# Linear attention with a Fourier mix and an MLP on one core: single PSUM banks, fixed rings, transposes by DMA for two batches, and a new order

## The chip, the core and the metric

The kernel runs on one core of one Trainium2 chip. A core has five engines that run their own instruction streams: TensorE (PE in the profile), VectorE (DVE), ScalarE (ACT), GpSimd (POOL) and SyncE (SP), and 16 DMA engines that they share. The metric is the time of one execution on the device in microseconds; the median of the runs is compared. Lower is better.

## What is computed

The reference is a linear attention with a decaying state, then a Fourier mix over sequence and width, a normalisation and an MLP with residual. Batch B = 4, H = 8 heads, S = 768 tokens, D = 48, so a width of 384; the MLP is 1536 wide.

```python
for t in range(S):                              # per batch and head
    cur = einsum('bhd,bhe->bhde', u[None] * kt, vt)
    y[:, :, t] = einsum('bhd,bhde->bhe', rt, state + cur)
    state = w[None, :, :, None] * state + einsum('bhd,bhe->bhde', kt, vt)
...
X = np.real(fft(fft(x, axis=1), axis=2))        # x: y with the heads side by side
u = x + X
un = (u - mean(u)) / sqrt(var(u) + 1e-06)
out = u + maximum(un @ w_ch1, 0) @ w_ch2
```

Inputs r, k, v, w, u and both weights are f32, and so is the output.

## The kernel before

**Attention.** The tokens are cut into 24 chunks of 128, six to a batch. For chunk i, `load` brings k, r and v from HBM as [128 tokens, 8 heads, 48], so each contiguous run is 192 bytes (lines 270, 274, 276). `attend` multiplies k and r by powers of the decay (KR, line 290), turns k and r from token-major to feature-major with eight PE transposes (line 302) into one PSUM tile and copies this to SBUF (KRT, line 305 on ACT or 306 on DVE), forms products for the bonus term u (PR, line 307), the scores (A_ps, line 317), their causal mask (MA, on POOL after an ACT copy, lines 324 and 326, or on DVE, line 329), the state update (u_ps, line 349; Sst, lines 361 and 363), and in yd_ps the bonus (line 381), the carried state (line 386) and the masked scores by V (line 403). DE (line 392) and TT (POOL, line 394) make the bonus term; it joins either through PE (line 409) and an ACT copy, or in the DVE addition (line 412). The result of a chunk is X. The state carries from chunk to chunk inside a batch.

**Fourier.** For batch 0 the halves of X are folded chunk by chunk (`narrow`, lines 426 and 433), for the other batches once all six chunks are there (`fold`, lines 449, 455, 463: each EO and HH is one DVE instruction over three chunks). `fourier` multiplies by tables of cosines (te, tn; line 495), copies to SBUF (TT2, lines 504 and 507), reverses (TR, line 514), multiplies by the second table (line 533), adds X (UF: by a PE matmul with the identity, line 544, and ACT, line 552, or in one DVE instruction, line 546), rescales (UB, lines 555 and 559) and gathers the statistics (lines 563 and 565). A batch has two halves of three blocks. UB is turned to UNT: for batch 0 by PE (line 574), for the others by a DMA transpose issued from SP (line 601).

**MLP.** There are eight halves `hf`. `mlp1` makes twelve PSUM tiles of three matmuls each (line 618), each passed through the ReLU to HT by ACT (line 623) or DVE (line 626). `mlp2` makes three tiles of twelve matmuls (line 638), added to UF on DVE (osb, line 646) and written out from POOL (line 650). W1 and W2 are read as f32 and cast to bf16 by six DMAs issued from POOL (line 671), W1 after X of chunk 3 and W2 after X of chunk 5.

**Order.** `op` records every step with the engine or engines that can do it. `ORDER`, a string written out in the kernel, lists numbers of these steps, with `.1` where the second engine is taken. `emit` issues them in that sequence, so each engine's own stream, and SP's and POOL's queues of DMAs too, run in the order of the string. SP issues the loads one after the other, and a load waits where its buffer is not yet free. 150 `idle` matmuls are declared and 40 are listed (line 198); they only keep PE busy. PSUM has eight banks, shared out as rings: `mm` 3, `A_ps` 2, `tp`, `u_ps` and `yd_ps` one each (with `tp` of two kilobytes). SBUF tiles come from pools with a number of buffers each.

Of the kernel before, what the change touches and what calls it, by code (L numbers as in the profile page):

```python
# [11 lines left out]
AX = mybir.AxisListType  # L12
# [3 lines left out]
B = 4  # L16
H = 8
S = 768
D = 48
# [4 lines left out]
NP = H // 2  # L24
CH = 98

# [25 lines left out]
class _Tile:  # L52

    def __init__(self, source, ring, bufs):
        self.source, self.ring, self.bufs = source, ring, bufs
        self.value = None
# [5 lines left out]
class _Schedule:  # L62

    def __init__(self):
        self.ops = []

    def tile(self, source, ring, bufs):
        return _Tile(source, ring, bufs)

    def op(self, name, eng, ns, fn, r=(), w=(), new=(), use=(), after=(), dma=0, pri=0, port=False, other=(), fill=False,  # L70
           link=None, uses=None, fixed=False):
        alts = [(eng, ns, port, fn)] + list(other)
        self.ops.append(dict(name=name, alts=alts, deps=list(r), after=list(after), w=list(w), new=list(new),
                             use=list(use), dma=dma, pri=pri, fill=fill, n=len(self.ops), link=link,
                             uses=uses or [[] for _ in alts], fixed=fixed))

    def emit(self, order):
        counts = {}
        for n, a in order:
            o = self.ops[n]  # L80
            for t in o["new"]:
                if isinstance(t.source, list):
                    m = counts.get(t.ring, 0)
                    counts[t.ring] = m + 1
                    t.value = t.source[m % t.bufs]
                else:
                    pool, shape, dtype, name = t.source
                    t.value = pool.tile(shape, dtype, name=name, bufs=t.bufs)
            o["alts"][a][3]()
# [3 lines left out]
154 153 194 150 155 168 157 160 162 195 151 161 159 196 169 177 156 188 199 176 174 197 191 175 163 158 200 178 173 170 171 198 180 172 164 201 179  # L93
165 202 182 166 203 152 181 167 0 205 183 1 271 206 2 184 211 273 190 185 193 186 293 187 204 3 207 4 274.1 5 208 272.1 294 295 275 209 276 296.1 212
283 281 277.1 279 6 297 7 216 8 282.1 278.1 280 9 10 210 284 315 298 268 303 269 11 301.1 299 302.1 285 317 214 304.1 12 318.1 215 300 287 286 13 288
320 337 305 321.1 323 14 15 16 316 192 324 339 217 189 306 325 322.1 338 307 218 17 18 340 19 326 213 309.1 308 319 219 347 310.1 341 342 359 348.1
327 345.1 343.1 20 21 328 346.1 329 361 22 344.1 362 331.1 330 23 381 24 332.1 364 402 349 360.1 220 367.1 383 363 350 365 221 369 368.1 351 25 26 270
231 27 384.1 366 353.1 352 222 386 385 354.1 226 289 28 312 370.1 387.1 389.1 371 1006 334 227 290 29 311 30 372 388.1 31 373 32 33 390.1 34 1007
375.1 374 333 35 291 376.1 36 1005 335 37 292 391 378 377 743 355 757 392 764 356 313 336 382 358 380 225 379 357 420 314 393 765 766 228 767 768 744
401 395 394 745 746 747 758 759 396 223 403 411 397 1009 224 760 404 398 761 400 399 1008 419 748 769 762 749 1010 406 770.1 763 229 750 751 409.1 752  # L100
405 753 412.1 230 754 755 410.1 421 756 429 413 422.1 407 773 774.1 771 779 414 775.1 772 424 780 781 415 785 776 427.1 799 786 787 811 408 782 800
812.1 417.1 801 805 813.1 416 806 807 795 788 793 794 796.1 797 798 425 38 39 802.1 1011 418.1 808.1 428.1 426 819 814 1017 456.1 820.1 423 1012 437
431 1018 823 1033 432 824 438 232 439 433 1034.1 821 474 233 1027 440.1 435 822.1 1015 1028 455 1035 1016 442 1036 441 1039 443.1 444.1 445 1037 492
1019 446 1040.1 1038 434 240 1013 1020.1 430.1 237 1051 436 1014 246 447 1052.1 449 1049 243 450 448 451 1023 1050 783 465 1024 457 473 466.1 1025
453.1 458.1 241 452 1026 1029 235 454.1 459 460 777 1030 236 475 461.1 463.1 778 467 242 784 476 1021 462.1 1061 491 1022 1031 1062 1043 477 247 1032
464.1 248 468 493 515 478 494 1044 552.1 238 481 495 239 1055 789 469 479 234 790 809 496 791 482 471 470 792 480 499.1 1056 1045 497 570 472 498 1053
534 1057 1046 485 1054 252 1041 815 1058 486 483 487 1067 1042.1 484.1 803 489.1 488 804 816 1068 810 490.1 533 817 501 588 1065 818 1069 502 267 503
1063 1066 500.1 255 517 1064 1070 505 1059 518.1 504 1047 1060 506 520 1048 507 535 523.1 521 1091 508 536 509 1092 516 510 258 1079 1093 522 511 1080
1094 512 513 1103 1081 514 1082 1104 551 825 829 1105 826 827 830 831 828.1 1106 837 838 832 839 553 524.1 840 833 834 841 835 554 538 836.1 525 541.1
842 843 526.1 844.1 519 855 537 849 845.1 856 857 850.1 527 543 851.1 864 846.1 876 858 852.1 870 544 871.1 877.1 528 863 865.1 539 605 561 866.1  # L110
542.1 529 607 878.1 556 867.1 531 872.1 879.1 530 559.1 560.1 540 557 1073 532 873 1071 558 1075 884 1072.1 1074 545 1076 562 1099 546 1077 555 1100
569 1087 1078 1083 1088 847 547 579 244 1084 1107 580 245 608 1085 1108.1 250 1095 859 1086 251 571 1096.1 1097 253 549.1 572.1 548 1098 254 1119
550.1 587 262 574 1120 563 263 1101 573 575 256 853 589 564 577 565 1089 257 1102.1 1111 590.1 1090 576 567 566 1115 1112 591 630 568 578 592 264 848
854 581 860 593.1 595 594.1 1116 582 609 861 1127 862 583 1117 874 596 585 584 1128 648 586 1118 720 880 599 249 1135 1129 600 601 261 1133 1136 868
1113 1134 1130 869 603 602 881 1114.1 1137 1109 604 1138 597 875 1125 606 1110.1 610 684 598 1123 882 647 613 615 1139 616 611 883 614 1124.1 1126
1140 617 612 619.1 1121 1141 618 629 1131 1122 1142 620.1 1175 259 1132 621 631 260 622 1176 265 632 623 266 1163 1177 624 1178 634 1164 637.1 638.1
635 625 1151 1165 636 628 1152 1166 626 627 639 649 1153 640.1 885 886 633 1154 887 650 897 898 888.1 899 889 890 900.1 891 657 641 892 893 651 894
895 652 642 901 896 683 655 903 904.1 909 902 905.1 915 643 910 911 916.1 685 917.1 906.1 645 644 924 912.1 653 930 918.1 931.1 666.1 923 936 686 646
654 937.1 925.1 659 665 926.1 688 932.1 687 667 927.1 938.1 668.1 656 1143 939 669 1147 919 1144 1145 1148.1 660 1155 661 1146 658 1159 1156 701 663
675 691 1149 1173 689 1150.1 692 662 1174 670 690 664 1160 703 676 677 673 1161 704.1 678 1169 671 679 1162.1 1157 1170 705 681 706 1158 913 672 1167  # L120
709 907 674 1199 1168 908 710 914 707 920 680 934 1171 921 708 682 1187 933 922 702 1172.1 944 695 719 1200 696 940 697 721 693 722.1 699 698 694.1
1188 1201 711 700 1202 724 712.1 1189 713 727.1 725.1 1179 714 728.1 715 1195 1180 726.1 1181 1196 1190 717 716 723 1197 1182 718 1185 1198 928 729
1191 1186.1 730 731 1211 1192.1 929 733 935 732 941 1212 942 734 735 1183 1205 1213 1184 736 1206 1203 1214 1193 1204 737 1209 1194 738 1207 1210 1247
739 1208 741 1248 742 740 943 945 957 1249 946 947 958 959 1250 948.1 949 950 960 951 953 954 952.1 955 1235 956 961 962 1236 963 1237 964.1 975 965.1
969 1238 976 977 970.1 1223 971.1 966.1 978.1 972.1 984 967 996 983 985 997.1 1224 986 998.1 988 987 1225 999 989 990 1226 979 991.1 1215 968 992.1
1000 1243 1216 993.1 1221 994 1004 1244 1245 995 1222 1217 980 973 1246 1231 974 1218 1233 1001 1232.1 981 1227 1002 1234.1 1219 1228 1003 1251 982
1220 1253 1252 1265 1254 1239 1266 1267 1240 1269 1268 1241 1270 1281 1242 1229 1282 1275 1230 1279 1276 1255 1280 1271 1256.1 1257 1272 1258 1283
1273 1274 1284 1277 1285 1263 1278 1286 1259 1264 1287 1291 1260 1292 1261 1262 1288 1293 1294 1295 1289 1290 1296 1297 1298
"""


def _order(sch):
    return [(int(t.split(".")[0]), int(t.split(".")[1]) if "." in t else 0) for t in ORDER.split()]


@with_exitstack
def kernel(
    ctx: ExitStack,
# [54 lines left out]
    def new(pool, shape, dtype, name, bufs):  # L193
        return sch.tile((pool, shape, dtype, name), name, bufs)
# [524 lines left out]
```

## Time and profile before

| what | value |
|---|---|
| median of 3 runs | 198.49 us (198.18 to 200.11) |
| span of the profiled execution | 196.4 us, first to last instruction |
| median less span | 2.1 us |
| PE busy | 170.4 us, 87% |
| DVE busy | 148.6 us, 76% |
| ACT busy | 112.2 us, 57% |
| POOL busy | 60.5 us, 31% |
| granted PE clock, mean | 0.982 |
| HBM read, written | 20.03 MB, 4.72 MB |

The profile gives its own execution by the span; what lies around it is taken as the 2.1 us between the span and the median. A group of instructions is shown as line, engine, operation, output and inputs, shape and count, then busy us and mean ns of one, then the engine's idle time ahead of it and what ended that. The row of slices gives tenths of busy time in 40 equal pieces of the span. In the table by stretches each engine has its busy us and, in brackets, its instructions. A chain of waits is followed back from the last instruction; each piece is a start, a length and what it was.

### The profile page before, as it was taken

The numbers are of one execution on the slowest core, as the hardware profiler recorded it, in microseconds if no ns is written. First come the engines' busy times: TensorE is split into PE (matmuls) and PEld (weight loads), VectorE is DVE, ScalarE is ACT, GpSimd is POOL, SyncE is SP. The second block draws the span as 40 slices with busy tenths as digits, with TensorE's granted clock in tenths as the row PEclk, the third lists the DMA queues.
The fourth block names the chain that finished last, engine by engine and source line by source line (L and its number), as shares of the span: only waits on it lengthen the run. The fifth ranks groups of instructions, "written<-read, shape, count | busy, mean of one in ns | idle before, by whom it ended". The sixth has DMA issues, their size and how long they took to land.

```text
span 196.4 us, 4461 instructions
## 1 busy us (share of the span) xinstructions
PE 170.4 (87%) x1711; PEld 113.8 (58%) x1711; DVE 148.6 (76%) x334; ACT 112.2 (57%) x263; POOL 60.5 (31%) x90
## 2 busy tenths in 40 slices
PE   0698993399699999997999999979999998899990
PEld 0355651387467666685566665866676576555650
DVE  7789994167889998989898979998888969702140
ACT  3956650259687767168765643786934526693100
POOL 5034260333211453315126253434724111000131
PEclk9999999669999999999999999999999999999999
DMA  5999999899998994323799455230032114400221
GB/s 99 202 213 216 249 178 218 173 186 189 189 220 165 205 216 101 82 83 62 141 194 198 136 122 122 80 60 3 2 63 80 40 43 100 100 0 3 80 105 55
DMA packets 86404, 24.43 MB, mean 124 GB/s; under 512 B 82928, under 2 KB 84592, under 8 KB 86384
## 3 DMA queue, kind: packets, MB, share of 16 engines
q1 hardware_dynamic: 81520, 16.69, 43.8%
q0 software_dynamic: 3680, 7.08, 13.8%
q10 hardware_dynamic: 1184, 0.39, 1.0%
q8 instruction: 13, 0.21, 0.5%
q14 instruction: 7, 0.06, 0.1%
HBM read 20.03 MB, written 4.72 MB: 126 GB/s over the span
## 4 chain that ended last, share of the span: by engine, by line
PE 49%; DMA 20%; issue 19%; POOL 3%; DVE 3%; ACT 2%; SPq 1%; POOLq 0%; DVEq 0%
PE mm L618 15%; PE mm L638 14%; DMA vt<-in_v_dram 11%; PE tp L302 5%; DMA UNT<-UB 3%; DMA kr<-in_r_dram 3%; PE mm L495 3%; PE A_ps L317 3%; DMA te_t<-te_c 3%; POOL out_dram L650 2%; PE yd_ps L403 2%; PE mm L533 2%; PE u_ps L349 1%; PE yd_ps L386 1%; DVE KR L290 1%
## 5 line engine op out<-in xcount | busy, mean ns | idle before, releaser
L618 PE MATMUL mm<-UNT,W 128*128 128x384 bf16 x288 | 53.5, 326 | 2.6 <-DMA UNT<-UB 2.6
L638 PE MATMUL mm<-W,HT 128*128 128x384 bf16 x288 | 51.0, 326 | 0.0
L623 ACT ACTIVATE HT<-mm 128x384 bf16<-128x384 f32 x75 | 36.4, 492 | 18.1 <-PE mm L618 18.0
L394 POOL TENSOR_TENSOR TT<-V,DE 128x384 bf16<-128x384 bf16 x24 | 22.8, 951 | 57.1 <-ACT DE L392 28.6
L638 PEld LDWEIGHTS <-HT 128*128 128x128 bf16 x288 | 27.2, 98 | 16.8
L618 PEld LDWEIGHTS <-W 128*128 128x128 bf16 x288 | 26.0, 97 | 18.3 <-DMA UNT<-UB 3.1
L650 POOL DMA_DIRECT2D out_dram<-osb x24 | 13.4, 557 | 48.6 <-DVE osb L646 45.0
L326 POOL TENSOR_SCALAR_AFFINE_SELECT MA<-AC 128x512 bf16<-128x512 bf16 x27 | 18.3, 684 | 25.2 <-ACT AC L324 13.9
L646 DVE SCALAR_TENSOR_TENSOR osb<-mm,rstd,UF 128x384 f32<-128x384 f32 x24 | 14.8, 615 | 12.8 <-PE mm L638 12.3
L290 DVE TENSOR_TENSOR KR<-kr,wtab 128x768 bf16<-128x768 f32 x24 | 23.4, 975 | 0.5 <-DMA kr<-in_r_dram 0.2
L626 DVE TENSOR_SCALAR HT<-mm 128x384 bf16<-128x384 f32 x21 | 11.6, 554 | 9.8 <-PE mm L618 9.5
L324 ACT CAST AC<-A_ps 128x512 bf16<-128x512 f32 x27 | 15.6, 588 | 5.1 <-PE A_ps L317 5.1
L198 PE MATMUL mm<-zero 128*128 128x512 bf16 x40 | 12.6, 416 | 6.8 <-DVE eps_t L231 6.8
L302 PE MATMUL tp<-ident,KR 128*128 128x128 bf16 x192 | 16.0, 231 | 0.9 <-DVE KR L290 0.5
L302 PEld LDWEIGHTS <-KR 128*128 128x128 bf16 x192 | 13.0, 104 | 5.0 <-DVE KR L290 3.2
L412 DVE TENSOR_TENSOR X<-yd_ps,TT 128x384 bf16<-128x384 f32 x15 | 8.3, 553 | 8.5 <-POOL TT L394 6.8
L329 DVE TENSOR_TENSOR MA<-A_ps,mtri 128x512 bf16<-128x512 f32 x21 | 14.0, 680 | 0.6 <-PE A_ps L317 0.5
L305 ACT COPY KRT<-tp 128x1024 bf16<-128x1024 bf16 x11 | 11.1, 1013 | 5.5 <-PE tp L302 5.3
L403 PE MATMUL yd_ps<-V,MA 128*128 128x48 bf16 x192 | 8.8, 184 | 6.2 <-ACT V L296 6.2
L296 ACT CAST V<-vt 128x384 bf16<-128x384 f32 x19 | 9.3, 513 | 8.4 <-DMA vt<-in_v_dram 8.3
L495 PE MATMUL mm<-te_t,XF 128*128 128x193 bf16 x108 | 13.4, 261 | 0.5 <-DVE XF L433 0.5
L403 PEld LDWEIGHTS <-MA 128*128 128x128 bf16 x192 | 8.2, 97 | 9.7 <-issue 7.3
(81 smaller groups left out, 247.7 us busy)
## 6 DMA issues: line engine op xcount, KB each, us to landing
kr<-in_k_dram SPq DMA_DIRECT2D x24, 192.0 KB, 3.9
vt<-in_v_dram SPq DMA_DIRECT2D x24, 192.0 KB, 3.9
out_dram<-osb POOLq DMA_DIRECT2D x24, 192.0 KB, 2.2
kr<-in_r_dram SPq DMA_DIRECT2D x23, 192.0 KB, 3.8
W<-in_moe_w_ch_dram POOLq DMA_DIRECT2D x6, 384.0 KB, 7.6
te_t<-te_c SPq DMA_DIRECT2D x1, 579.0 KB, 5.1
hid_t<-hid_c SPq DMA_DIRECT2D x1, 288.0 KB, 5.2
wrow<-in_w_dram ACTq DMA_DIRECT2D x1, 192.0 KB, 3.8
```

What stands on the lines that cost most here:

```text
L290: op(("KR", i), "DVE", 960, lambda: nc.vector.tensor_tensor(out=KR().rearrange("t s p (a d) -> t (s p) a d", a=2)[:, :, :, 0:D], in0=kr(). ...
L302: nc.tensor.transpose(tp()[:, s, p, :], KR()[:, s, p, :], ident)
L324: op(("AC", i, a), "ACT", 590, lambda: nc.scalar.copy(AC(), A_ps[a]()), r=[("A", i)], w=[("AC", i, a)], new=[AC], use=[A_ps[a]], pri=pri, ...
L326: op(("MA", i, a), "POOL", 630, lambda: nc.gpsimd.affine_select(out=MA[a](), in_=AC(), pattern=[[0, NP], [1, 128]], base=0, channel_multip ...
L394: op(("TT", i), "POOL", 830, lambda: nc.gpsimd.tensor_tensor(out=TT(), in0=V(), in1=DE().unsqueeze(2).to_broadcast([128, H, D]), op=AluOp. ...
L403: nc.tensor.matmul(y[:, h, :], lhsT=MA[a]()[:, p, :], rhs=V()[:, h, :], start=False, stop=(h == H - 1), skip_group_check=True)
L495: nc.tensor.matmul(fp()[:, par, :], lhsT=lhsT[:, g * CH:g * CH + 128], rhs=rhs, start=(nb == 0 and par == 0), stop=(nb == last and par == ...
L618: nc.tensor.matmul(hp(), lhsT=W1[:, dt, ft * 128:(ft + 1) * 128], rhs=UNT()[:, :, dt, :], start=(dt == 0), stop=(dt == 2))
L623: op(("HT", hf, ft), "ACT", 495, lambda: nc.scalar.activation(out=HT()[:, ft, :], in_=hp(), func=Act.Relu, scale=-1.0), r=[("hp", hf, ft)] ...
L638: nc.tensor.matmul(mo(), lhsT=HT()[:, ft, j * 128:(j + 1) * 128], rhs=W2[:, ft, :], start=(ft == 0), stop=(ft == 11))
L646: op(("osb", hf, j), "DVE", 620, lambda: nc.vector.scalar_tensor_tensor(out=osb(), in0=mo(), scalar=rstd()[:, j:j + 1], in1=UF()[:, j, :], ...
L650: op(("out", hf, j), "POOL", 550, lambda: nc.gpsimd.dma_start(out=out[b, row:row + 128, :], in_=osb()), r=[("osb", hf, j)], w=[("out", hf, ...
```

## The change

It does the following.

- All eight PSUM banks are tiles of their own. The order string names a bank for each step that opens a PSUM tile (`150@4`), so any use can take any bank.
- SBUF tiles are rings of fixed tiles; UF goes from 5 to 4 buffers and UNT from 4 to 3.
- Queries of batch 0 are read by two DMAs, one from ACT and one from SP, six tokens to a row (runs of 1152 bytes), in place of six loads. They are scaled by six tables `wtq` (ACT) in two DVE instructions (QR6), turned by 24 PE transposes (`tq6`) and copied to QT6 by four copies (three on ACT, one on DVE). Chunks 0 to 5 then have k only in KR, four transposes and half a KRT copy. QR6 lies in the bytes of W2, and the queries and `wtq` in two of the HT tiles.
- Chunks 12 to 23 (batches 2 and 3) get KRT by a DMA transpose from SP in place of eight PE transposes and a copy.
- W1 is loaded in two blocks of columns, and `mlp1` waits for the block it needs; its place is set by POOL's order alone. W2 may be loaded after `tq6`.
- EO and HH of `fold` are split by chunk, so each pair of chunks can start when it is there. The parts of yd_ps and of `mlp2` (four parts of three matmuls in place of two of six) are steps of their own.
- Outputs go from POOL or from SP: 11 and 13 in the new order.
- Only the padding of KR is set to zero; some of these go to POOL.
- `ORDER` is another string. Choices in it: KRT copies on DVE 4 (13), masks on DVE 28 (21), UF on DVE 18 (8), UB on DVE 6 (14), X on DVE 11 (15), identity matmuls for UF 6 (16) and for the bonus 13 (9); idle matmuls 42 (40); the numbers before are in brackets. W1 stands on POOL after TT of chunks 9 and 7, W2 after TT of chunk 13 and the masks of chunk 16.

The diff, cut to its core (the order strings are left out):

```diff
+NC = B * NQ
+SLOTS = 6
+XBAR_CHUNKS = frozenset(range(12, 24))
+XBAR_HALVES = frozenset(range(2, 8))
...
             for t in o["new"]:
-                if isinstance(t.source, list):
-                    m = counts.get(t.ring, 0)
-                    counts[t.ring] = m + 1
-                    t.value = t.source[m % t.bufs]
-                else:
-                    pool, shape, dtype, name = t.source
-                    t.value = pool.tile(shape, dtype, name=name, bufs=t.bufs)
-            o["alts"][a][3]()
+                if t.ring == "bank":
+                    t.value = t.view(self.banks[banks.pop(0)])
+                    continue
+                tiles = self.rings[t.ring]
+                m = counts.get(t.ring, 0)
+                counts[t.ring] = m + 1
+                t.value = tiles[m % len(tiles)]
...
+    sch.banks = [ps.tile([128, 512], F32, name=f"bank{i}") for i in range(8)]
...
+    q6 = HTs[2].rearrange("p f t -> p (f t)").bitcast(F32).rearrange("p (h j d) -> p h j d", h=H, j=SLOTS)
+    wtq = HTs[1].rearrange("p f t -> p (f t)").bitcast(F32).rearrange("p (j c) -> p j c", j=SLOTS)
+    QR6 = W2.rearrange("p f d -> p (f d)")[:, 0:SLOTS * NP * 128].rearrange("p (j q c) -> p j q c", j=SLOTS, q=NP)
+    QT6 = const([128, NP, S], BF16, "QT6")
...
+        for j in range(SLOTS):
+            one(("wtq", j), "ACT", "wt", lambda j=j: nc.scalar.activation(wtq[:, j, :], lw, Act.Exp, scale=jcol[:, j:j + 1]),
+                r=["lw", "jcol"])
...
+    def queries():
+        for hh in range(2):
+            hs = slice(hh * 4, hh * 4 + 4)
+            eng, q = ("ACT", nc.scalar) if hh == 0 else ("SP", nc.sync)
+            one(("q6", hh), eng, "dma_q6", lambda hs=hs, q=q: q.dma_start(
+                out=q6[:, hs], in_=r[0, hs].rearrange("h (p j) d -> p h j d", j=SLOTS)))
+            one(("QR6", hh), "DVE", "QR6", lambda hh=hh, hs=hs: nc.vector.tensor_tensor(
+                out=QR6.rearrange("p j q (a d) -> p (q a) j d", a=2)[:, hs, :, 0:D], in0=q6[:, hs],
+                in1=wtq.rearrange("p j (h d) -> p h j d", h=H)[:, hs], op=AluOp.mult),
+                r=[("q6", hh), "QR0"] + [("wtq", j) for j in range(SLOTS)])
+        for p in range(NP):
...
+                for j in range(SLOTS):
+                    nc.tensor.transpose(tq()[:, j, :], QR6[:, j, p, :], ident)
...
+            op(("QT6", p), [("ACT", "QT6", lambda p=p, tq=tq: nc.scalar.copy(
+                QT6[:, p, :].rearrange("c (t j) -> c j t", j=SLOTS), tq())),
...
+            if i in XBAR_CHUNKS:
+                one(("KRT", i), "SP", "xbar8", lambda: nc.sync.dma_start_transpose(
+                    out=KRT().rearrange("d s p t -> d (s p) t"), in_=KR().rearrange("t s p c -> t (s p c)")),
+                    r=[("KR", i)], new=[KRT], use=[KR])
...
+        def seq(h, n, alu):
+            one(("EO", b, h, n), "DVE", "EO", lambda: nc.vector.tensor_tensor(
+                out=EO()[:, h, n, :], in0=X()[:, n, :], in1=X()[:, 3 + n, :], op=alu),
+                r=[("X", b * NQ + n), ("X", b * NQ + 3 + n)], new=[EO] if h == 0 and n == 0 else [], use=[EO, X],
+                after=[("EO", b, 0, 0)] if h or n else [])
...
+        for s in range(4):
+            one(("mo", hf, j, s), "PE", "mo3", lambda s=s: mm(3 * s, 3 * s + 3),
+                r=[("HT", hf, ft) for ft in range(3 * s, 3 * s + 3)] + [("W2", 3 * s // 4), ("W2", (3 * s + 2) // 4)]
+                + ([("mo", hf, j, s - 1)] if s else []), new=[] if s else [mo], use=[HT, mo])
...
+        op(("out", hf, j), [("POOL", "dma_out", lambda: nc.gpsimd.dma_start(out=out[b, row:row + 128, :], in_=osb())),
+                            ("SP", "dma_out", lambda: nc.sync.dma_start(out=out[b, row:row + 128, :], in_=osb()))],
...
-    weights("W1", lambda n: w1[n * 128:(n + 1) * 128, :], lambda n: W1[:, n, :], [("X", 3)], 1870, -90)
+    for n in range(2):
+        one(("W1", n), "POOL", "dma_w1", lambda n=n: nc.gpsimd.dma_start(
+            out=W1[:, :, n * 768:(n + 1) * 768], in_=w1[:, n * 768:(n + 1) * 768].rearrange("(c p) f -> p c f", p=128)))
+    for n in range(3):
+        one(("W2", n), "POOL", "dma_w2", lambda n=n: nc.gpsimd.dma_start(
+            out=W2[:, n * 4:(n + 1) * 4, :], in_=w2[n * 512:(n + 1) * 512, :].rearrange("(f p) d -> p f d", p=128)),
+            after=[("tq6", p) for p in range(NP)])
```

## The prediction, made before the changed kernel ran

> **What bounds the kernel now.** I read the 40 slices of the page first, then the busy time of each engine in five stretches, then the chain of waits in order of time, then the DMA queues by stretch, and last the groups that the change takes away.
>
> ```profile
> PE   0698993399699999997999999979999998899990
> PEclk9999999669999999999999999999999999999999
> DMA  5999999899998994323799455230032114400221
> ```
> TensorE is full nearly everywhere but in the first quarter, where the DMA row is full instead; in slices 8 and 9 the granted clock falls to 0.6.
>
> ```profile
> 0.00:49.40 49.40, 34.55 (x389) 23.38 (x390) 36.18 (x99) 27.17 (x60) 16.34 (x27) 0.93 1.03 192
> 49.40:110.00 60.60, 57.34 (x624) 38.74 (x624) 54.67 (x111) 40.97 (x99) 21.01 (x29) 1.00 0.75 157
> 110.00:148.50 38.50, 37.16 (x419) 25.63 (x415) 34.46 (x69) 24.62 (x61) 16.64 (x24) 1.00 0.28 68
> 148.50:166.20 17.70, 17.61 (x150) 12.09 (x146) 14.59 (x34) 8.02 (x21) 2.71 (x5) 1.00 0.17 54
> 166.20:196.40 30.20, 23.77 (x146) 14.01 (x144) 8.68 (x23) 11.45 (x26) 3.78 (x7) 1.00 0.20 61
> ```
> The columns are length, then busy us of PE, PEld, DVE, ACT and POOL, the clock, the DMA share and GB/s. The stretches end at the first MLP matmul (49.4), about the last chunk of batch 2 (110) and of batch 3 (148.5), and the last product of the second transform of batch 3 (166.2). Up to 49.4 DMA is the bound (1.03). From there to 166 it is PE, 112.1 busy of 116.8 us, with DVE close behind (103.7). After 166 only MLP is left.
>
> ```profile
> 25.89 11.20 DMA vt<-in_v_dram
> ...
> 40.48 11.14 DMA vt<-in_v_dram
> ...
> 89.43 3.33 DMA UNT<-UB
> ...
> 129.54 3.22 DMA UNT<-UB
> ```
> From the chain (start, length): two loads of v take 11 us each, because the weights' reads share the DMA engines with them. PE sat idle 6.2 us before line 403 for the first. The transposes through DMA land after 3.2 to 3.3 us.
>
> **What the change takes from PE.** I matched each number of the two order strings to its call by counting the calls.
>
> ```profile
> L302 PE MATMUL tp<-ident,KR 128*128 128x128 bf16 x192 | 16.0, 231 | 0.9 <-DVE KR L290 0.5 <-DVE KRT L306 0.3
> ...
> L305 ACT COPY KRT<-tp 128x1024 bf16<-128x1024 bf16 x11 | 11.1, 1013 | 5.5 <-PE tp L302 5.3
> ...
> L306 DVE COPY KRT<-tp 128x1024 bf16<-128x1024 bf16 x13 | 8.9, 686 | 2.6 <-PE tp L302 2.5
> ...
> L544 PE MATMUL mm<-X,ident 128*128 128x384 bf16 x16 | 4.9, 334 | 0.0
> ```
> Matmuls overlap, so I cost them by their place in the chain: eight transposes 0.45 us, three matmuls of 384 columns 0.487, A 0.33, u 0.17, one of 384 columns 0.165. The useful work of before adds up to 152.4 us. Batches 2 and 3 lose their transposes: 12 x 0.45 = 5.4. Batch 0 has six times four and four times six in place of six times eight, the same 48. L544 goes from 16 to 6 (-1.65), L409 from 9 to 13 (+0.65). After: 146.0.
>
> **DVE and ACT.** The DVE rows add up to 162.1 us where DVE is busy 148.6, as their ends overlap; I scale by 0.917. Terms: KRT copies 13 to 4 (-6.2), UB 14 to 6 (-3.4), KR of batch 0 at half size (-2.8), X -2.2, V and TT2 -2.3, memsets of the pads alone and partly on POOL (-2), against UF 8 to 18 (+6.4), masks 21 to 28 (+4.8), QR6 +2.9, the folds in thirds +1.5, S, QT6 and the rest +1.7. Sum -1.6, after 160.5, or 147.2 busy. ACT stays (123 by rows in both): fewer AC and UF, but six wtq (0.6 each) and three QT6 more. Not in the trace: QR6 (1152 products) is at least one KR (0.95), at most two (1.95), and by elements 1.45, which I take. QT6 lies between L305 by elements (0.76) and L504 by elements, also strided (1.2); I take 0.8. A third of a fold lies between 0.25 (L426 with 192 elements) and 0.40 (half of L455); I take 0.3. Pads on POOL: at L394's 2.5 ns per element under 2 us, hidden before the first query arrives; uncovered, they would hold QR6 by that much. `PSUM` banks given singly move no work: their gain or loss is the order's, and in the ranges.
>
> **DMA.**
>
> ```profile
> q0 software_dynamic: 432, 1.18, 52.2%
> ```
> ```profile
> q0 software_dynamic: 1584, 1.18, 52.9%
> ```
> ```profile
> q1 hardware_dynamic: 18859, 3.57, 100.9%
> ```
> ```profile
> q1 hardware_dynamic: 1184, 0.30, 38.5%
> ```
> These are (packets, MB, share of 16 engines) the first weights in 25 to 37 us, the second in 37 to 52, the loads in 52 to 70, and one transpose of UB in 129 to 133. So W1 costs 0.522 x 12 = 6.3 us of the whole DMA, W2 7.9, a load of 1024 packets 0.986 (18.16 us / 18859), and a transpose of 0.295 MB 1.54 us. W1 in column blocks (768 rows, between the two) 6.8: +0.5. Queries of batch 0: six loads, 5.9 us, become 1.18 MB in rows of 1152 B. The page "DMA: Bandwidth & Descriptors" (Specifications) asks for 512 B or more for line rate and gives 435 GB/s as the ceiling, which would make it 2.7 us. By the trace, te and hid (rows of 2304 and 4632 B) took the remainder of 10 to 25 us: 15.5 us less 13227 short packets (12.7), 2.8 us for 0.87 MB, 311 GB/s; 3.8 us. I take the trace: -2.1, not -3.2. Twelve KRT transposes are new: 8/9 of 1.54 = 1.37 each. The same page (Latency and other measured facts) has 261 GB/s for a transpose, 1.0 each; the trace has 0.295/1.54 = 192 GB/s. That is 16.4 us of DMA against 12; the trace decides. It falls where DMA was 0.28 to 0.75 busy. SP also needs 1.29 us to issue each, which its waits cover (it waits some 48 us before line 601 alone). Thirteen outputs go from POOL (0.56 each, 7.2 us less there, where 48.6 us are idle before outputs anyway) to SP: six of them stand before the last second-transform product, each waiting for its DVE op, with v(19) to v(23), KRT of chunks 19 and 21 to 23 and UNT behind; uncovered, 0.6 each and the wait. I cost it at nothing, since those loads run chunks ahead.
>
> **The front, to the first MLP matmul.** QR6 waits for six wtq after wt: ACT's exponentials start 0.52 us apart from 5.17 on, so 5.17 + 7 x 0.52 = 8.8, and the queries land about 8 to 9. DVE has only 4.5 us of work ahead of QR6, so it idles about 4.7. Up to the point of the order where the MLP begins, DVE has 43.6 us busy (36.0 before), ACT 43, PE 26.9 (18.9 before). With 1.5 us of small waits (of before's 13.2 idle us some 2 lie outside the first v load): 43.6 + 4.7 + 1.5 = 49.8. The weights say the same. On POOL W1 is queued behind TT of chunk 9, whose DVE work ends at 35.0 + 4.7 + 1 = 40.7; then 6.8 us of transfer, some 1 us of other loads and 2 us to land: 50.5. The half that comes first helps little, since the third MLP matmul group needs the other. So the MLP begins about 50.5, hardly other than 49.4, but with 8 us more PE work behind it. The stall on v(5) goes: v(5) is now the tenth load or so of SP, due before 20 us, and te comes after batch 0.
>
> **From there.** Order sums of after, PE / DVE busy: to the last chunk of batch 2, 32.6 / 34.7; to that of batch 3, 36.0 / 35.9; to the last second-transform product, 16.0 / 15.7; the rest, PE 34.4. The longer in each: 34.7 + 36.0 + 16.0 = 86.7. Before, the same stretch had 109.6 of PE and took 116.8, 6.6% more. Now two engines are even, and W2 is late: POOL reaches it after TT of chunk 13, PE wants its first block after about 5.4 us and its last after 10.9, where the three transfers need 7.9 plus about 4 of transposes and loads between; some 2 us wait. I take 8%: 93.5. At the end PE has MLP alone, 34.4; from its last matmul (191.1) to the end 5.3 as now. The outputs moved to SP wait behind nothing there. **Span 50.5 + 93.5 + 34.4 + 5.3 = 183.7** against 196.4. The median of the runs lies 2.1 above the span now (198.49), so **185.8, given as 186**.
>
> **Rivals.** *The order holds* (0.12): waits of 2% (88.4) and an MLP at 48.5 give 176.6 + 2.1 = 179. For it: PE was full in 49 to 110. Against: there only one engine was full. *DVE keeps its share* (0.22): to 166.2 DVE is busy 139.9, 84.2%. If after's 129.8 also take 84.2%, the MLP rest begins at 154.2, the span is 193.9, the time 196. For it: a fixed order passes every DVE delay on. Against: 11 us of its idle time were the load of v. *The transposes come late* (0.12), slower: KRT by PE came 0.45 + 1.0 after KR; by DMA 3.2 on an empty queue, and it stands on SP behind loads. The page named above (Queues, rings and completion order) says that each engine takes descriptors in ring order; the 11.2 us load shows what a full queue does. Then A, its masks and y wait, and SP's next loads behind a transpose that waits for KR. It decides from 12.7 + 2.0 = 14.7 us, or 1.23 us of PE wait per transpose; at 1.4 it is 16.8, 202.6. Against: DMA has room after 70 us, and other work stands between. Forecast (0.54): own range 181 to 191.
>
> **How the numbers follow.** A run can tell about 1% from no change, 196.5 to 200.5. The faster side has all of the first case and the forecast and two thirds of DVE's (0.81); its top and the late case's bottom give 0.08; the rest of the late case 0.11. The range 178 to 199 leaves out some 0.05 of the first case below and 0.12 above.
>
> **What would show it.** PE without a gap over 3 us after 15 us and at full clock; line for tp at 12 groups; the first MLP matmul at 48 to 53; DVE over 90% between; KRT by DMA landing in 3 to 5 us. Wrong if A waits for KRT over 1 us each time, if W1 or W2 stop PE over 5 us, or if the MLP begins after 56.

## The result, and the profile after

The median went from 198.67 us (four runs, 198.18 to 200.11) to 187.32 us: a ratio of **0.939 [0.932, 0.947]**, some 12 us less by the ratio. The forecast was 186. The profiled execution took 187.45 us, its span is 185.7, so 1.75 us lie around it (2.1 before). One of its four runs, 194.95 us at a lower clock, is left out of the ratio; in the experiments runs of this kind are left out of the ratios and of comparisons too, though not of the medians.

The rows of slices of the changed kernel:

```profile
PE   7983687799996999899899989999999999999990
...
ACT  2799989979994599959205477566432265102310
...
PEclk9998599999997899999999999999999999999998
DMA  5999299898996937999999999995111413201033
```

The row of ACT before, which was not shown above:

```profile
ACT  3956650259687767168765643786934526693100
```

Counted from 1, TensorE (PE) now has its holes in slices 4, 5 and 13. ACT is full in slices 3 to 5, with gaps in PE and then, in slice 5, in DMA beside it: a new limit. DMA is busy to slice 27: seven transposes of KRT, the second weights and three more loads fall in 80 to 125 us, where DMA had been half empty. The stretches, with the columns of the table before: up to the first MLP matmul, to the last product of the second transform, to PE's end, the tail.

```profile
0.00:54.15 54.15, 43.86 (x537) 29.49 (x537) 43.70 (x107) 46.23 (x99) 19.17 (x33) 0.94 0.91 186
54.15:146.80 92.65, 87.97 (x866) 59.44 (x867) 81.66 (x213) 54.61 (x140) 26.49 (x35) 0.98 0.84 158
146.80:180.93 34.13, 34.13 (x211) 20.33 (x208) 16.26 (x39) 9.93 (x23) 2.71 (x5) 1.00 0.20 67
180.93:185.70 4.77, 0.00 (x0) 0.00 (x0) 0.69 (x2) 0.00 (x0) 0.54 (x1) 0.85 0.33 125
```

Before, the first two took 49.4 and 116.8 us and the rest 30.2. So the front grew by 4.8 us but does 9.3 us more of PE's work, the middle lost 24.1, the rest grew by 8.7 as more of MLP stands there. Work has moved from stretch to stretch, so their lengths don't show where time was won; PE's idle time does. It was 14.9, 4.7 and 6.4 us in front, middle and rest, and is 10.3, 4.7 and 4.8 now. PE's busy time fell by 4.4 (170.4 to 166.0), and the two together are the span's 10.7: in sum, what went of the waits lay in the front and at the end, nothing in the middle. (Busy time counts the `idle` matmuls, 12.6 us before and 14.0 now.) The chain of waits (start, length) names the new holes:

```profile
48.36 9.34 DMA W<-in_moe_w_ch_dram
74.55 4.69 DMA UNT<-UB
...
86.13 5.98 DMA W<-in_moe_w_ch_dram
```

W1's second block is on the chain, and it was issued late: POOL came to the first block after the bonus term of chunk 9, at 46.8, and to the second at 48.4. What had held that up is in the groups (busy us, mean ns of one, idle before):

```profile
L367 ACT COPY QT<-bank 128x768 bf16<-128x768 bf16 x3 | 7.8, 2867 | 0.4 <-PE bank L364 0.4
L369 DVE COPY QT<-bank 128x768 bf16<-128x768 bf16 x1 | 2.7, 2705 | 1.7 <-PE bank L364 1.7
L355 DVE TENSOR_TENSOR W<-HT,HT 128x1152 bf16<-128x1152 f32 x2 | 2.7, 1346 | 0.0
```

A QT6 copy takes 2.87 us on ACT and 2.71 on DVE, where I had 0.8. Three of them in a row stop ACT from 12.2 to 20.0, and PE waits for them three times; the first scores run at 20.76:

```profile
15.00 0.49 PE L364 MATMUL bank<-ident,W 128*128 128x128 bf16 x6 [1.49 <-ACT QT L367]
17.55 1.01 PE L412 MATMUL bank<-ident,KR 128*128 128x128 bf16 x8 [2.06 <-ACT QT L367]
20.10 0.58 PE L273 MATMUL bank<-zero 128*128 128x512 bf16 x1 [1.53 <-ACT QT L367]
```

(PE in order of time: start, length, in brackets the wait ahead.) The granted clock was low as well, 0.85 in 10 to 20 us and 0.81 in 20 to 30.

### The profile page after: what moved, and what is told of

It is laid out like the page before. It is cut to its first block, busy times and chain, and to the rows that moved or that the text cites. A ratio compares the mean times of both kernels' runs of the same rounds, so it can differ in the third digit from the quotient of the medians.

```text
span 185.7 us, 4285 instructions
## 1 busy us (share of the span) xinstructions
PE 166.0 (89%) x1611; PEld 109.3 (59%) x1611; DVE 142.3 (77%) x359; ACT 110.8 (60%) x260; POOL 48.9 (26%) x74
## 4 chain that ended last, share of the span: by engine, by line
issue 29%; PE 23%; DMA 16%; DVE 12%; ACT 8%; POOL 7%; SPq 3%; POOLq 0%; DVEq 0%; ACTq 0%
PE bank L745 10%; DMA W<-in_moe_w_ch_dram 8%; PE bank L765 4%; ACT QT L367 4%; DMA wuc<-in_w_dram 3%; DMA UNT<-UB 3%; PE bank L635 2%; POOL out_dram L776 2%; DMA vt<-in_v_dram 2%; POOL TT L534 2%; DVE KR L399 2%; DVE PR L450 2%; DVE HH L568 2%; DVE MA L472 2%; PE bank L460 2%
## 5 line engine op out<-in xcount | busy, mean ns | idle before, releaser
L745 PE MATMUL bank<-UNT,W 128*128 128x384 bf16 x288 | 57.7, 333 | 3.6 <-DMA W<-in_moe_w_ch_dram 2.1
L750 ACT ACTIVATE HT<-bank 128x384 bf16<-128x384 f32 x76 | 34.4, 493 | 37.2 <-PE bank L745 36.9
L765 PE MATMUL bank<-W,HT 128*128 128x384 bf16 x288 | 54.2, 326 | 0.8 <-DMA W<-in_moe_w_ch_dram 0.5
L469 POOL TENSOR_SCALAR_AFFINE_SELECT MA<-AC 128x512 bf16<-128x512 bf16 x20 | 14.3, 723 | 39.7 <-ACT AC L467 35.9
L751 DVE TENSOR_SCALAR HT<-bank 128x384 bf16<-128x384 f32 x20 | 10.9, 554 | 14.7 <-PE bank L745 14.7
L472 DVE TENSOR_TENSOR MA<-bank,mtri 128x512 bf16<-128x512 f32 x28 | 18.4, 679 | 0.6 <-PE bank L460 0.6
L772 DVE SCALAR_TENSOR_TENSOR osb<-bank,rstd,UF 128x384 f32<-128x384 f32 x24 | 14.3, 607 | 3.6 <-PE bank L765 2.3
L273 PE MATMUL bank<-zero 128*128 128x512 bf16 x42 | 14.0, 479 | 2.8 <-ACT QT L367 1.5
L698 DVE BATCH_NORM_STATS2 st<-UF 128x6 f32<-128x384 f32 x24 | 12.7, 545 | 0.1
L467 ACT CAST AC<-bank 128x512 bf16<-128x512 f32 x20 | 11.5, 590 | 1.6 <-PE bank L460 1.4
L635 PE MATMUL bank<-te_t,XF 128*128 128x193 bf16 x108 | 11.7, 247 | 0.2 <-DVE XF L574 0.2
```

The costliest lines, as they stand in the source:

```text
L273: op("idle", [("PE", "idle", lambda: nc.tensor.matmul(z(), lhsT=zero[:, 0:128], rhs=zero, start=True, stop=True))], r=["zero"], new=[z])
L467: op(("AC", i, a), [("ACT", "AC", lambda: nc.scalar.copy(AC(), A_ps[a]())), ("NONE", "", None)], r=[("A", i)], w=[("AC", i, a)], new=[AC], ...
L469: op(("MA", i, a), [("POOL", "MA", lambda: nc.gpsimd.affine_select(out=MA[a](), in_=AC(), pattern=[[0, NP], [1, 128]], base=0, channel_mul ...
L472: ("DVE", "MA", lambda: nc.vector.tensor_tensor(out=MA[a](), in0=A_ps[a](), in1=mtri.unsqueeze(1).to_broadcast([128, NP, 128]), op=AluOp.m ...
L635: nc.tensor.matmul(fp()[:, par, :], lhsT=lhsT[:, g * CH:g * CH + 128], rhs=rhs, start=(nb == 0 and par == 0), stop=(nb == last and par == ...
L698: one(("st", b, blk), "DVE", "st", lambda: nc.vector.bn_stats(out=st(), in_=UF()[:, j, :]), r=[("UF", b, blk)], new=[st], use=[UF])
```

## The experiments

The "changed kernel" is the one after the change.

**The copies of the queries.** Theory: the scattered writes of QT6 make them slow, and delay the front as a whole.

```diff
-QT6[:, p, :].rearrange("c (t j) -> c j t", j=SLOTS), tq()
+QT6[:, p, :].rearrange("c (t j) -> c t j", j=SLOTS), tq().rearrange("c j t -> c t j")
```

> The four copies of the turned queries write PSUM to SBUF with the element order of the target (unit steps on the write side, steps of 256 bytes on the read side), nothing else. Theory: the 12-byte steps of the writes make a copy take 2.7 to 2.9 us; written in order it takes 0.8 to 1.2, the first scores come at 14 to 16 us in place of 20.8, the MLP begins 3 to 6 us earlier, time 182 to 185. Rival: the cost is in the two-byte elements taken apart from each other, on whichever side the steps lie; then the copies stay at 2.7 us or more and the time at 187.

Measured: 183.65 us, ratio **0.920 [0.910, 0.930]** to before. The groups of that kernel:

```profile
L367 ACT COPY QT<-bank 128x768 bf16<-128x768 bf16 x3 | 2.2, 807 | 0.3 <-PE bank L364 0.3
L369 DVE COPY QT<-bank 128x768 bf16<-128x768 bf16 x1 | 1.0, 958 | 0.1
```

```profile
0.00:48.63 48.63, 42.32 (x534) 28.95 (x536) 41.60 (x107) 40.91 (x99) 18.98 (x33) 0.96 0.97 199
48.63:140.90 92.27, 86.75 (x866) 58.88 (x867) 81.71 (x213) 54.55 (x139) 26.71 (x35) 1.00 0.86 163
140.90:175.10 34.20, 34.19 (x211) 20.35 (x209) 16.26 (x39) 9.93 (x23) 2.70 (x5) 1.00 0.20 67
175.10:179.80 4.70, 0.00 (x0) 0.00 (x0) 0.69 (x2) 0.00 (x0) 0.54 (x1) 1.00 0.34 127
```

The theory was right. Between these two profiled executions ACT's three copies save 5.6 us, the first stretch 5.5, the span 5.9; the other three stretches stay within 0.4. So the delay went through the fixed order about undiminished. The ratios (0.939 and 0.920) are some 4 us apart; the runs of the new kernel that count are 181.6 to 184.3, and the profiled one is the fastest of them. It is the write side, since the read has the large step now. That step is not free on every engine, as the contiguous copies of the same kernel show:

```profile
L440 ACT COPY KRT<-bank 128x1024 bf16<-128x1024 bf16 x2 | 2.0, 1016 | 0.0
L441 DVE COPY KRT<-bank 128x1024 bf16<-128x1024 bf16 x4 | 2.6, 680 | 0.1
```

By elements 768 of them would take 0.76 us on ACT and 0.51 on DVE, beside 0.81 and 0.96 with the step; why DVE loses more, no run here tells. Two more kernels ask what made the writes slow, by writing two or three neighbours at a time:

```diff
+QT6[:, p, :].rearrange("c (t a j) -> c a t j", a=3, j=2), tq().rearrange("c (a j) t -> c a t j", j=2)
```

> The changed kernel with the QT6 copies written in pairs of neighbouring elements (4 bytes together, then a step to 12 bytes further), in place of single elements 12 bytes apart. It asks what made those copies slow (2.87 us on ScalarE, 2.71 on VectorE, against 0.81 and 0.96 in order). Theory by the page SBUF - State Buffer (Door 1): a line of SBUF has 16 bytes, and two accesses in a row to a line reach full speed; in pairs 256 writes of a pass go to 96 lines, 2.7 a line, so the copies take 0.8 to 1.1 us on both, and the time is that of the copies in order, ratio 0.91 to 0.93. Rival: each break in the sequence of addresses costs the same, 384 breaks in place of 768: 0.81 + 2.06 x 384/768 = 1.8 us on ScalarE, 0.96 + 1.75/2 = 1.8 on VectorE, the time between the two, some 185.

> As with pairs, but three neighbouring elements at a time (6 bytes), 256 breaks. By the 16-byte line: 0.8 to 1.0 us on both engines. Rival, a price for each break: 0.81 + 2.06 x 256/768 = 1.5 us on ScalarE, 1.5 on VectorE, the time some 184 to 185.

Measured, pairs and then triples:

```profile
L367 ACT COPY QT<-bank 128x768 bf16<-128x768 bf16 x3 | 2.3, 834 | 0.4 <-PE bank L364 0.4
L369 DVE COPY QT<-bank 128x768 bf16<-128x768 bf16 x1 | 1.0, 958 | 0.1
```

```profile
L367 ACT COPY QT<-bank 128x768 bf16<-128x768 bf16 x3 | 2.8, 1032 | 0.4 <-PE bank L364 0.4
L369 DVE COPY QT<-bank 128x768 bf16<-128x768 bf16 x1 | 1.0, 1019 | 0.1
```

Pairs still break the sequence of addresses 384 times and cost 0.03 us or nothing; the rival, a price for each break, had 1.8 us for them and 1.5 for triples. The rule of the Trainium skill's page "SBUF — State Buffer" (Door 1), lines of 16 bytes and at least two accesses to each for full speed, agrees with single elements and pairs: single elements 12 bytes apart hit a line 1.3 times, pairs 2.7 times. What the page draws from it, that one can stride over 8 bf16 for free, does not: a step of 6 took 3.5 times as long on ACT. Nor does the rule as it stands give the triples, which hit a line four times and took 0.22 us more than in order on ACT; some of them straddle two lines, which may be why, but no run tells. Against another rival, that a half-written word of 4 bytes is what costs, stands L643 (L504 before): it writes single bf16 elements 4 bytes apart, 386 of them in 0.61 us, or 1.2 for 768 by elements. The ratios are 0.920 [0.909, 0.931] and 0.910 [0.904, 0.916], both as with the copies in order.

**W1 in time.** The MLP's first wait is for W1. W1's two loads were put right after TT of chunk 0 (in the changed kernel), or a few places ahead (with the copies in order), and then v of chunk 10 ahead of k and r of its chunk as well.

```diff
-... 465 1053 486.1 497 438 849.1 454 1054 484.1 ...
+... 447 1053 450 461@1 ... 492 1054 847@5 ...
```

(1053 and 1054 are the two blocks of W1, 454 is TT of chunk 7, 447 the mask of chunk 7, 492 TT of chunk 9; the lines are those of the second of the three kernels.)

> Both DMAs of the first weights move on POOL from behind TT of chunks 9 and 7 to right behind TT of chunk 0; the rest as in the changed kernel. Theory: the MLP waits for the second block of columns (57.75 us, 1.8 us of PE idle, and PE idles from 55.6), and DMA has room at 20 to 30 us (0.67 busy), so the MLP runs from 52 to 54 us on and the time is 184 to 186. Rival: the weights take the DMA engines from the loads of chunks 6 to 9, which come 5 to 7 us later; no gain or a loss, 187 to 191.

> The changed kernel with the QT6 copies written in order, and both W1 blocks a few POOL places earlier: the first after the mask of chunk 7 (some 3.8 us earlier, near 37.3), the second after TT of chunk 9 (some 1.6 us earlier). With the copies in order alone, the MLP began at 48.6 and waited for the second W1 block until 52.1 (0.5 and 1.6 us of TensorE's idle time). Theory: these 2.1 us are W1's place, the loads that it passes now are not due soon, and so the wait goes: first MLP matmul 48 to 49, no wait over 0.5 us for the second block, the time some 1 to 2 us under the copies alone: 181.5 to 183. Rival: as when both blocks went to the very front, the DMA engines are full there (share 1.0), and what W1 gains is taken from loads of k, r and v: a new wait of 1 to 3 us between 38 and 50, 183 to 187.

> The changed kernel with the QT6 copies in order, W1 a few places earlier, and the load of v of chunk 10 moved ahead of k and r of chunk 10 on SyncE. With W1 earlier the MLP's wait for W1 was gone, but ScalarE waited 1.9 us for this v (it landed 7.7 us after its issue, beside W1), and the first MLP matmul ran at 50.2, not at 48.6. Theory: that wait is what W1's move cost; with v first the MLP begins at 48.5 to 49.5, 180.5 to 181.5. Rival: k and r of chunk 10 then come late in its place, since the DMA engines are full to about 52 us: no gain, 182 to 184.

Measured: 189.56 us, ratio 0.950 [0.943, 0.957], for the first; the rival was right. Its waits from 20 to 60 us (total, times, longest) show a new one in place of W1's:

```profile
PE bank L437 <- DVE KR L399: 4.0, 1, 4.0
DVE KR L399 <- DMA kr<-in_r_dram: 3.7, 1, 3.7
```

The second: 182.14 us, in the theory's range, but 0.911 [0.904, 0.918] against 0.920 [0.910, 0.930] with the copies alone is no difference that these runs can tell. The wait for W1 is gone, but the first MLP matmul runs at 50.2, not 48.6, as the chain of waits has a load of v in its place:

```profile
37.22 7.69 DMA vt<-in_v_dram
44.94 0.51 ACT V L404
```

The third: 183.85 us, 0.910 [0.902, 0.919]. That wait for v is gone as well, and the MLP still begins at 50.1. The rival had k and r late in its place, but this is the only wait for a load in 30 to 55 us:

```profile
DVE KR L399 <- DMA kr<-in_r_dram: 0.3, 1, 0.3
```

So in the first two kernels a transfer moved ahead made another one late, as the rivals said; in the third, where the theory failed too, no load holds the front up and it is no shorter. VectorE is busy 9.70 of the 10 us from 40 to 50 there, so its own work is the likely limit; no run tests it.

**Column blocks of W1.** First only the list of what each MLP step needs was changed, with both blocks for all; then W1 was read in three blocks of rows, as before the change.

> The changed kernel with the QT6 copies written in order, and every first-layer MLP matmul waiting for both W1 blocks: the change's column blocks undone in their effect, at the same place of the queue. Theory: in the version with the copies alone the first MLP matmul ran at 48.6 and the second block landed in time for 52.1; eighteen matmuls of the first block (six tiles of 0.49 us, 2.9 us) ran before that, with attention between. Without them the first MLP matmul moves to about 52 and TensorE idles some 2 to 3 us more: 185.5 to 187. Rival: the order has attention work close behind that TensorE would do anyway only in its turn, and the delay is made up or is no more than the 1.6 us already lost: 183 to 184.5.

> The changed kernel with the QT6 copies written in order and W1 in three blocks of rows, as before the change: two where its first block of columns stood, one where its second stood. A tile of the first MLP layer needs all three, where a block of columns was enough for six tiles. The run in which only the list of needs was changed turned out to be the same instructions as the copies alone (the waits come from the parts of a tile that overlap), so it tells nothing of this; its MLP went on at 53.1 after the second block. Theory: the first two tiles, some 1 us of TensorE's work, move behind that landing, and the row blocks are 0.5 us cheaper to transfer: between 0.5 us better and 1.5 us worse than the copies alone, 182 to 185, first MLP tile complete near 52.5 to 53.5. Rival: the column blocks are what lets attention and MLP run side by side at the start; without them the order's waits chain up and it costs 3 us or more: 186 or over.

The first told nothing of its question: the list only serves the planning, and the instructions were those of the copies in order. As a repeat it shows how far the ratios of one kernel agree: 0.913 [0.907, 0.919] against 0.920 [0.910, 0.930]. With rows: 183.94 us, 0.918 [0.912, 0.925], the theory's. PE waited 1.93 and 1.61 us for W1 in its profile (at a lower clock just there, down to 0.5 in a slice) and completed the first tile near 52.5. Column blocks bring nothing that can be measured here.

**The order of the loads alone,** in the kernel before: v of chunks 4 and 5 ahead of v of chunk 6 and the tables, W2 after TT of chunk 7.

> The kernel before with the order of its transfers alone changed: v of chunks 4 and 5 ahead of v of chunk 6 and of the MLP tables, W2 after TT of chunk 7. It stalled for v of chunk 4 (6.2 us of TensorE before the masked scores by V) and of chunk 5, because the weights' reads shared the DMA engines with them. Theory: that stall is what the change's front won; moved alone it gives back 4 to 8 us: 190.5 to 195. Rival: up to 49 us the DMA engines are full (share 1.03), so another transfer becomes late in its place, W2 or the loads of chunks 6 to 9, and the time stays: 196.5 to 202.

Measured: 195.07 us, ratio **0.980 [0.973, 0.987]**, some 4 us of 199 (2.6 to 5.4 by the interval), the low end of the theory. The first MLP matmul moved from 49.4 to 46.6, but ScalarE still waits for v (in 20 to 50 us; the kernel before, then this one):

```profile
ACT V L296 <- DMA vt<-in_v_dram: 7.6, 1, 7.6
```

```profile
ACT V L306 <- DMA vt<-in_v_dram: 4.3, 1, 4.3
```

So a third or so of the change's 12 us can be had without any of its other parts, and by moving transfers among full DMA engines (share 0.97 up to 46.6 us), which brought nothing above. Which of the moves did it is not parted.

**The DMA transposes alone,** in the kernel before, for chunks 12 to 23, at the place where the order had the copy to KRT; once from SyncE and once from ScalarE. And the reverse, the changed kernel with eight PE transposes and a copy (in turn on ACT and DVE), in free banks at the place of the DMA transpose.

```diff
-op(("tp", i), "PE", 450, transposes, ...)
-op(("KRT", i), "ACT", 1010, lambda: nc.scalar.copy(KRT(), tp()), ...
+op(("KRT", i), "SP", 1300, lambda: nc.sync.dma_start_transpose(out=KRT()..., in_=KR()...), ...
```

> The kernel before, with only one part of the change: chunks 12 to 23 get KRT by a DMA transpose from SP where the copy stood in the order. Theory: PE is the bound from 50 to 166 us, 5.4 us of its work go, and the later landing (3.2 us and the queue against 1.5) gives some back: 193 to 197. Rival: the transposes arrive late, A and its followers stall PE by over 1 us each: 199 or more.

> As the kernel before with DMA transposes alone for chunks 12 to 23 (212.9, ratio 1.068), but issued from ScalarE at the place of the KRT copy, not from SyncE. Loads and UNT no longer stand behind a transpose that waits for KR or for a free KRT buffer. Theory that the queue on SyncE cost most of the 14 us (it waited 11 us for KR and 4 for KRT buffers there): 199 to 205. Rival, that the later landing costs it (3 to 5 us from KR to KRT in an order made for 1.5 us; TensorE waited 14 to 16 us for KRT there): 208 to 215, with TensorE's wait for KRT still over 12 us.

> The changed kernel with that one part undone: eight PE transposes and a copy (in turn on ACT and DVE) for chunks 12 to 23, in free banks, where the DMA transpose stood. Theory: PE has 5.4 us more and DVE 4: the time rises by 5 to 7 us to 192 to 194. Rival: the DMA transposes were worth nothing, since DVE and DMA set the pace: 186 to 189.

From SyncE: 212.89 us, ratio **1.068 [1.060, 1.076]**. The rival was right. Its waits:

```profile
PEld L326 <- DMA KRT<-KR: 16.1, 6, 3.8
PE A_ps L326 <- DMA KRT<-KR: 14.3, 6, 3.4
```

The twelve landed 3.0 to 5.4 us after their issue and the scores stood right behind them. From ScalarE it was 223.99 us, 1.121 [1.110, 1.131], worse than with SyncE and above the ranges of theory and rival. PE's waits for KRT are as long as before, as the rival had it:

```profile
PE A_ps L326 <- DMA KRT<-KR: 15.3, 6, 6.5
```

So freeing SyncE's queue of them does not help. But this run doesn't part queue from landing cleanly, since the transposes of UB stayed on SyncE and now waited for ScalarE's:

```profile
SPq L610 <- DMA KRT<-KR: 34.7, 7, 7.2
```

In the changed kernel the same transposes cost hardly a wait; SyncE's landing times there are 2.7, 3.6 and 4.2 us (least, median, most), and these are all the waits for them on DVE (PE has 0.3 us, before its weight loads):

```profile
DVE PR L450 <- DMA KRT<-KR: 1.4, 2, 1.1
```

Put back to PE, the changed kernel took 198.65 us (one run; its median is 201.9), some 11 us more than the changed kernel's 187.45, where the theory had 5 to 7 and the rival nothing. PE is busy 4.3 us more (170.3 against 166.0), so some 7 us of the span's 11.2 (196.9 against 185.7) are waits. The order wasn't made for them, so this is not the transposes' own worth, and neither is the loss in the other direction.

## Why the prediction was right, and by which errors

The sum, term by term (us):

| term | predicted | changed kernel | with copies in order |
|---|---|---|---|
| to the first MLP matmul | 50.5 | 54.15 | 48.63 |
| from there to the last second-transform product | 93.5 | 92.65 | 92.27 |
| the rest of MLP | 34.4 | 34.13 | 34.20 |
| from the last matmul to the end | 5.3 | 4.77 | 4.70 |
| span | 183.7 | 185.7 | 179.8 |

The columns of the two kernels are one profiled execution each.

**One term was mis-sized: QT6.** I took 0.8 us a copy, near the low end of 0.76 (L305, in order) to 1.2 (L504, "also strided"). L504 writes bf16 with a step of 4 bytes and so hits a 16-byte line four times; QT6's step is 12 bytes. The right row was in my hands, the wrong property of it: the step in bytes, not that there is one. A copy took 2.87 us. In all it cost 5.6 us of ACT and 1.7 of DVE, 5.9 of the span between the two profiled executions, and some 4 by the ratios. None of the rivals had it.

**The front had a second error of the other sign.** With the copies at the duration that I had assumed, it took 48.6, not 50.5. In the changed kernel QR6 (1.346 us, 1.45 forecast) and DVE's idle time ahead of it (0.64 + 1.87 + 2.20 = 4.7, as forecast) were right, and with the copies in order TT of chunk 9 came at 40.3 (40.7). But "the half that comes first helps little" made me let the MLP begin after the whole of W1; it begins with the first block. The second was there only for 52.06, 1.6 us later than I had the whole, and PE's wait for it (1.64) belongs to the next term.

So QT6's 5.9 us, less 1.9 in the front, 1.2 in the middle and 0.8 at the ends, leave 2.0 us of span: 185.7 against 183.7. The median, with other runs and less time around the span, is 187.3 against 186. That the errors nearly cancel is luck; a number that is right to 1% is no proof of its terms.

**The middle** held as a sum: 92.65 us, 6.9% over my 86.7, where I took 8%. Its picture of two engines that are even did not. PE was busy 87.97 us of it, 95% (its order sums gave 84.6), DVE 81.66, 88% (they gave 86.3, and I had named 90%); so PE alone was near its limit. DVE came to 142.3 in all, not 147.2; I haven't followed which of its rows were smaller. W2 stopped PE for 0.50 us (some 2 forecast): W2's chain piece of 5.98 us is long, but other PE work lay under it. Two more of my signs failed: the MLP began at 54.15, outside 48 to 53, and PE's clock fell in 10 to 30 us.

**The KRT transposes**: landing (2.7 to 4.2 us, 3 to 5 forecast) and issue (1.25 us, 1.29 forecast) were about as predicted, and the rival of late transposes did not happen in this order. It did, with PE's waits of 14.3 us and all, as soon as they stood in the old one. I had it right that "other work stands between", and that is the whole of it.

**What stays open.** The singly given banks, the rings, the thirds of the folds and the choices of engine can't be undone one at a time, because each order names its banks and its engines. Only the loads (4 us) have been parted from the rest, and whether an order made anew without the transposes would do as well is not known. The outputs moved to SyncE, costed at nothing, were not tried either way.

## What to carry to other kernels

When a copy changes the layout, work out how many accesses in a row fall into one 16-byte line of the target, and try the loop order that puts the scattered side on the read; changing this one line made the kernel 0.920 of before instead of 0.939. A step handed from PE to DMA landed 2.7 to 5.4 us after its issue here: without other work behind it, as in the old order, it made the kernel 7% slower. While the DMA engines are full, moving a transfer ahead can only move the wait to another one (twice here), or win 2.8 us at the first MLP matmul (in the old order): look at what the transfers that it passes are needed for. And where work moves between stretches, compare the idle time of the engine that is full, not the lengths.

## What the hardware showed that I had not expected

A copy of 128x768 bf16 from PSUM to SBUF: written in order 0.81 us on ACT and 0.96 on DVE, in steps of 12 bytes 2.87 and 2.71, in pairs 0.83 and 0.96, in triples 1.03 and 1.02. Reading the bank with a step of 128 elements cost 0.05 us on ACT and 0.45 on DVE, by an estimate from their contiguous copies (0.76 and 0.51 by elements). And transposes by DMA from two engines stood in each other's way in this program: those of SyncE waited 34.7 us in seven places for those of ScalarE. The page "DMA: Bandwidth & Descriptors" (Silent corruption) has a rule that two such streams must not be in flight at once; the program's waits agree with it, and what the chip would do without them no run here shows.
